# Attention scores of the later batches: float32 products on host-transposed queries and keys in place of split float16 ones

## The chip, the cores and the metric

The kernel runs on one core of a Trainium2 chip. The metric is the device time of one execution in microseconds (us), median of several runs; the kernel before has 992.15 us, from three runs between 989.74 and 999.76 us. One further execution was recorded by the hardware profiler, and all rows below come from it.

## The reference: what is computed

There are 8 batches of 8 heads, 576 tokens and 64 elements per head. Keys and values are averaged over groups of 8 tokens, which leaves 72 of each; attention over those 72 gives a 576 x 512 matrix per batch, and a feed-forward block of width 2048 follows.

```python
k_p = k.reshape(B, H, Sp, pool, D).mean(axis=3)          # pool = 8, Sp = 72
v_p = v.reshape(B, H, Sp, pool, D).mean(axis=3)
scores = scale * np.matmul(q, k_p.transpose(0, 1, 3, 2))
attn = softmax(scores)                                    # over the 72 keys
x = np.matmul(attn, v_p)                                  # heads side by side: 576 x 512
xn = (x - mu) / np.sqrt(var + 1e-06) * g_ln
out = x + np.maximum(xn @ w_ch1, 0.0) @ w_ch2             # 512 -> 2048 -> 512
```

## The kernel before, in words

The 8 x 576 = 4608 tokens are cut into 36 tiles of 128 tokens, numbered t = 0 to 35, and into 9 chunks of four tiles (512 tokens) for the feed-forward block. A batch is 4.5 tiles long, so tiles 4, 13, 22 and 31 belong to two batches each; `segments` gives the one or two ranges of a tile with their batch. These four are called split tiles below, the other 32 whole tiles.

Attention for a tile has two stages. `stage_a(t)` loads the queries of tile t+2, computes scores (`scores`), exponentials (`probs`, which ends in a DMA transpose), and, for the tiles after the first nine, prepares the queries of tile t+1 (`split_q`). `values(t)` multiplies by the pooled values, normalises, and produces the transposed input of the feed-forward block. `ffn_in` (L488) and `ffn_out` (L515) are the two large products; each is done as three float16 products over high and low parts, with a 128x512 product as the unit, and one call of either is a unit of 12 such products.

The scores have two forms. In the first two batches (tiles 0 to 8, `T32` = 9) the host has laid out the queries transposed, and L353 multiplies float32: one product takes a pair of heads, 128 rows of both heads' elements, against `kblk`, a block-diagonal 128x144 matrix with the 72 pooled keys of each head of the pair. A float32 product of the program is two matmul instructions in the trace. In the later batches (tiles 9 to 35) the queries come with tokens on the partitions. `split_q` finds the largest element of each row on VectorE (L326), derives a power of two from it (L107, L108, L114), combines it with the scale of the keys (L331), writes the high float16 part on ScalarE (L141) and the low part on VectorE (L142), and has a DMA transpose both (L335). The result lies in a `wf` buffer. Each head then takes two products, L348 with 128 rows against `KHH` and L349 with 64 rows against `KLL`, so a whole tile takes 16 matmuls and a split tile 32, where each covers 64 columns.

Keys are pooled on GpSimd by `pool_k`: L223 and L224 add halves, and the last addition goes to `kblk` in two half-height pieces (L228) for the first two batches, and to a `wf` buffer in one piece (L233) for the later ones. There `max_k` and `split_k` follow: a maximum (L237), a small matmul over all partitions (`all_max`, L129), a scale, a split, and six DMAs into the tile that serves as `KHH` and `KLL`.

`wf` is a pool of three buffers. Besides the split queries and keys, the conversion of the weights lives in it: the weights arrive in 16 blocks of 1 MB (`load_raw` into a ring of five buffers, L153), `convert` (L163 to L185) turns each into a float32 block in `wf`, and `split_w1` and `split_w2` write the high and low float16 weights from there. All transfers go through the queue of SyncE (SP).

Two things set the order. The text in `START` lists the operations up to the end of chunk 1: loads, pooling (`HK`), stage A of tiles 0 to 11 (`A`), values (`B`), weight conversion (`C`, `S1`, `M2`, `S2`) and feed-forward quarters (`I`, `O`). After it a loop over chunks 2 to 8 runs 32 feed-forward units each, with stage A of the next chunk's tiles ahead of units 0, 6, 12 and 18 (`A_AT`) and their values ahead of units 5, 11, 17 and 23 (`B_AT`); the keys and values of batch b are prepared behind the values of the last tile of batch b-2. The framework's scheduler simulates the program and may move instructions between engines' turns, so the order on an engine is not always that of the text.

Of the kernel before, what the change touches and what calls it, by code (L numbers as in the profile page):

```python
# [39 lines left out]
UNITS = 2 * NFT  # L40
B32 = 2
T32 = B32 * S // P
A_AT, B_AT = (0, 6, 12, 18), (5, 11, 17, 23)
# [16 lines left out]
@with_exitstack  # L60
def attn_ffn_kernel(ctx: ExitStack, tc: tile.TileContext, qT, q, kT, k, v, g, w1, w2, out):
    nc = tc.nc
# [21 lines left out]
    make_identity(nc, ident)  # L84
    kblk = [wk2.tile([P, NPAIR, 2 * KV], F32, name="kblk") for _ in range(B32)]
    phl = [const.tile([P, 2, H, P], F16, name=f"phl{i}") for i in range(2)]
# [9 lines left out]
    def wf_tile():  # L96
        return wk3.tile([P, NKT * WC], F32, name="wf")
# [4 lines left out]
    def scalar_tile(name, n=1):  # L102
        return small.tile([P, n], F32, name=name)
# [109 lines left out]

    KHH, KLL, CK, kst, kp, kmax, kraw = {}, {}, {}, {}, {}, {}, {}
    VA, VB, CV, vp, vmax, vraw = {}, {}, {}, {}, {}, {}

    def load_k(b, p, kr=None, queue=nc.sync):
        kraw[b, p] = kr = wk2.tile([P, POOL, KV], F32, name="kr") if kr is None else kr
        queue.dma_start(out=kr, in_=(kT[b] if b < B32 else k[b - B32])[:, p])

    def pool_k(b, p, eng):
        kr = kraw.pop((b, p))
        eng.tensor_add(out=kr[:, 0:4, :], in0=kr[:, 0:4, :], in1=kr[:, 4:8, :])  # L223
        eng.tensor_add(out=kr[:, 0:2, :], in0=kr[:, 0:2, :], in1=kr[:, 2:4, :])  # L224
        if b < B32:
            for j in range(2):
                r, c = slice(j * D, (j + 1) * D), slice(j * KV, (j + 1) * KV)
                eng.tensor_add(out=kblk[b][r, p, c], in0=kr[r, 0, :], in1=kr[r, 1, :])  # L228
        else:
            if p == 0:  # L230
                kst[b] = wf_tile()
                kp[b] = kst[b][:, 0 : NPAIR * KV].rearrange("p (a k) -> p a k", k=KV)
            eng.tensor_add(out=kp[b][:, p, :], in0=kr[:, 0, :], in1=kr[:, 1, :])  # L233

    def max_k(b):
        m = scalar_tile("mk")
        nc.vector.tensor_reduce(  # L237
            out=m, in_=kp[b], axis=AX.XY, op=ALU.max, apply_absolute_value=True
        )
        kmax[b] = all_max(m)  # L240

    def split_k(b):

        e, s = kmax.pop(b), scalar_tile("sk")
        kh, kl = (
            kst[b].bitcast(F16)[:, i * NPAIR * KV : (i + 1) * NPAIR * KV].rearrange(
                "p (a k) -> p a k", k=KV
            )
            for i in (2, 3)
        )  # L250
        kb = wk2.tile([P, NPAIR, 2 * KV], F32, name="kblk")
        kb = kb.rearrange("p a k -> p (a k)").bitcast(F16).rearrange("p (i h k) -> p i h k", i=2, k=KV)
        KHH[b], KLL[b] = kb[:, 0], kb[:D, 1]
        pow2_inverse(s, e, 13)
        CK[b] = wk3.tile([P, 1], F32, name="ck")
        nc.vector.tensor_scalar_mul(out=CK[b], in0=e, scalar1=2.0**-26 * EXP_SCALE)
        split(kp.pop(b), s, kh, kl)
        for j in range(2):
            r, hs = slice(j * D, (j + 1) * D), slice(j * NPAIR, (j + 1) * NPAIR)
            for i in range(2):  # L260
                nc.sync.dma_start(out=KHH[b][i * D : (i + 1) * D, hs, :], in_=kh[r])
            nc.sync.dma_start(out=KLL[b][:, hs, :], in_=kl[r])

# [36 lines left out]

    q_sb, ESC, E, PT, X, Z, zTs = {}, {}, {}, {}, {}, {}, {}

# [10 lines left out]
    def load_q(t):  # L313
        q_sb[t] = wk3.tile([P, NPAIR, P], F32, name="q")
        if t < T32:
            nc.sync.dma_start(out=q_sb[t], in_=qT[t])
        else:
            nc.sync.dma_start(out=q_sb[t].rearrange("p a c -> p (a c)"), in_=q[t - T32])

    def split_q(t):  # L320

        qn = q_sb.pop(t).rearrange("p a c -> p (a c)")
        flat = wf_tile().bitcast(F16)
        qhl = flat[:, 0 : 2 * DM]
        m, e, s = scalar_tile("mq"), scalar_tile("eq"), scalar_tile("sq")
        nc.vector.tensor_reduce(out=m, in_=qn, axis=AX.X, op=ALU.max, apply_absolute_value=True)  # L326
        pow2_floor(e, m)
        pow2_inverse(s, e, 13)
        ESC[t] = f = scalar_tile("esc")
        for r, b in segments(t):  # L330
            nc.vector.tensor_mul(out=f[r], in0=e[r], in1=CK[b][r])  # L331
        parts = qhl.rearrange("p (h a d) -> p h a d", a=2, d=D)
        split(qn.rearrange("p (h d) -> p h d", d=D), s, parts[:, :, 0, :], parts[:, :, 1, :])
        q_sb[t] = flat[:, 2 * DM : 4 * DM].rearrange("p (h c) -> p h c", c=P)
        nc.sync.dma_start_transpose(out=q_sb[t], in_=qhl)  # L335

    def scores(t):
# [4 lines left out]
        for half in range(2):  # L342
            ps = ps_s.tile([P, 512], F32, name="ps_s")
            for i in range(4 if t >= T32 else 0):
                h = 4 * half + i
                for r, b in segments(t):
                    o = ps[r, i * KV : (i + 1) * KV]
                    nc.tensor.matmul(o, lhsT=q[:, h, r], rhs=KHH[b][:, h, :], start=True, stop=False)  # L348
                    nc.tensor.matmul(o, lhsT=q[:D, h, r], rhs=KLL[b][:, h, :], start=False, stop=True)  # L349
            for i in range(2 if t < T32 else 0):  # L350
                p = 2 * half + i
                for r, b in segments(t):
                    nc.tensor.matmul(  # L353
                        ps[r, i * 2 * KV : (i + 1) * 2 * KV],
                        lhsT=q[:, p, r],
                        rhs=kblk[b][:, p, :],
                        start=True,
                        stop=True,
                    )
            pss.append(ps[:, : 4 * KV].rearrange("p (h k) -> p h k", k=KV))  # L360
# [11 lines left out]
    def probs(t):  # L372
        e, ph = E.pop(t), phl[t % 2]
        nc.scalar.activation(out=e, in_=e, func=AF.Exp, scale=ESC.pop(t) if t >= T32 else EXP_SCALE)
        nc.scalar.copy(  # L375
# [280 lines left out]
```

## Time and profile before

| what | before |
|---|---|
| median of 3 runs | 992.15 us (989.74 to 999.76) |
| the profiled execution, its own time | 994.91 us |
| its span, first to last instruction | 993.1 us |
| mean granted TensorE clock | 0.957 |
| TensorE matmul busy | 881.1 us (89%) |
| VectorE busy | 606.6 us (61%) |
| ScalarE busy | 294.0 us (30%) |
| GpSimd busy | 266.7 us (27%) |

In the rows, PE is TensorE's matmul side and PEld its weight loads, DVE is VectorE, ACT ScalarE, POOL GpSimd and SPq the DMA queue of SyncE. A row of a timeline has start and duration in us, engine, line, operation, output and inputs, a count when like instructions are merged, and in brackets the idle time of the engine just before with what ended it. A matmul's duration runs to its modelled end and overlaps the next one's; the distance from one start to the next is what it costs in a row of many. A row of groups has the count, the busy time and mean ns of one, and the idle time before them. A row of windows has the busy time and instruction count of PE, PEld, DVE, ACT and POOL in a stretch, then the granted TensorE clock (1.00 is full), the DMA share and GB/s.

### The profile page before, as it was taken

The page shows a single profiled execution, that of the slowest core. Times are in us where ns is not written, and L with a number is a line of the kernel's source. Part 1 is how long each engine was busy: PE and PEld are TensorE (multiplying, and loading weights), DVE is VectorE, ACT ScalarE, POOL GpSimd, SP SyncE. Part 2 cuts the span into 40 slices and gives each one's busy share as a digit, 9 for nine tenths or more (in the row PEclk, how much of TensorE's full clock was granted, in tenths as well). Part 3 has the DMA queues.
Part 4 walks back from the last instruction along what each step waited for, and adds up shares of the span by engine and source line. Part 5 has one row for each costly group of instructions (what it writes and reads, how often), then busy time and mean ns, then how long its engine had stood idle before and what let it go on. Part 6 is the DMA issues. An engine that isn't in the chain of part 4 may idle for free.

```text
span 993.1 us, 13139 instructions
## 1 busy us (share of the span) xinstructions
PE 881.1 (89%) x4826; PEld 442.8 (45%) x4826; DVE 606.6 (61%) x1540; ACT 294.0 (30%) x558; POOL 266.7 (27%) x316
## 2 busy tenths in 40 slices
PE   3135599584999999999999999999999999999998
PEld 2124346341444444445444444454444445444443
DVE  6999998858675467357636574676464435542222
ACT  3435443434322232223222222242232223210110
POOL 5865851326211623132402131211011101200000
PEclk9997799795999899999999899999998999999999
DMA  9848651533432564155324243323232212200001
GB/s 293 201 109 220 174 165 21 212 94 91 117 96 62 146 135 98 35 141 114 78 54 122 57 110 45 107 69 85 48 91 54 43 33 74 60 16 33 11 1 43
DMA packets 166001, 93.31 MB, mean 94 GB/s; under 512 B 144816, under 2 KB 148272, under 8 KB 163888
## 3 DMA queue, kind: packets, MB, share of 16 engines
q1 hardware_dynamic: 165936, 92.47, 36.4%
q8 instruction: 38, 0.62, 0.3%
q14 instruction: 27, 0.22, 0.1%
HBM read 45.09 MB, written 9.44 MB: 55 GB/s over the span
## 4 chain that ended last, share of the span: by engine, by line
PE 77%; DVE 14%; DMA 4%; issue 2%; SPq 1%; POOL 1%; ACT 1%; DVEq 0%; POOLq 0%; ACTq 0%
PE ps_f L515 35%; PE ps_f L488 34%; PE ps_s L349 3%; PE ps_s L348 3%; DVE wf L169 2%; DVE wf L166 1%; DVE w1L L142 1%; DMA q<-in_qT_dram 1%; DMA vr<-in_v_dram 1%; DVE y L458 1%; PE ps_x L413 1%; DVE a L455 1%; DVE e L365 1%; DVE wm L181 1%; PE ps_x L416 1%
## 5 line engine op out<-in xcount | busy, mean ns | idle before, releaser
L488 PE MATMUL ps_f<-zT,w1H 128*128 128x512 f16 (+1 forms) x1248 | 353.5, 368 | 6.7 <-DVE x L525 4.8
L515 PE MATMUL ps_f<-w2H,ring 128*128 128x512 f16 x1152 | 356.5, 385 | 0.8 <-DVE ring L497 0.8
L515 PEld LDWEIGHTS <-ring 128*128 128x128 f16 x1728 | 169.0, 99 | 204.2 <-issue 11.6
L488 PE MATMUL ps_f<-zT,w1L 128*128 128x512 f16 (+1 forms) x624 | 229.4, 368 | 0.0
L515 PE MATMUL ps_f<-w2L,ring 128*128 128x512 f16 x576 | 221.7, 385 | 0.0
L525 DVE SCALAR_TENSOR_TENSOR x<-ps_f,c_out,x 128x512 f32<-128x512 f32 x144 | 107.5, 748 | 137.3 <-PE ps_f L515 134.2
L488 PEld LDWEIGHTS <-w1H 128*128 128x128 f16 x1248 | 122.1, 99 | 131.7 <-issue 10.9
L497 DVE SCALAR_TENSOR_TENSOR ring<-ps_f,ring 128x512 f16<-128x512 f32 (+1 forms) x156 | 100.7, 647 | 117.5 <-ACT ring L496 116.3
L496 ACT ACTIVATE ring<-ps_f 128x512 f16<-128x512 f32 (+1 forms) x156 | 87.7, 564 | 246.4 <-PE ps_f L488 245.8
L382 POOL TENSOR_TENSOR phl<-e,phl 128x512 f16<-128x512 f32 x36 | 42.6, 1185 | 266.8 <-ACT phl L375 232.1
L488 PEld LDWEIGHTS <-w1L 128*128 128x128 f16 x624 | 62.0, 99 | 64.6 <-issue 2.2
L467 POOL TENSOR_TENSOR hl<-z,hl 128x512 f16<-128x512 f32 x36 | 42.5, 1180 | 147.5 <-ACT hl L466 140.0
L353 PE MATMUL ps_s<-kblk,q 128*128 128x144 f32 (+1 forms) x80 | 22.0, 457 | 52.0 <-issue 20.1
L436 ACT ACTIVATE x<-ps_x,rs 128x64 f32<-128x64 f32 x144 | 33.4, 315 | 115.4 <-DVE rs L427 58.6
L348 PE MATMUL ps_s<-kblk,wf 128*128 128x72 f16 (+1 forms) x240 | 50.9, 212 | 7.8 <-DMA wf<-wf 7.8
L349 PE MATMUL ps_s<-kblk,wf 64*128 64x72 f16 (+1 forms) x240 | 50.4, 210 | 0.0
L185 POOL TENSOR_TENSOR wf<-wf,ring 128x1024 f32<-128x1024 f32 x16 | 40.7, 2547 | 33.2 <-DMA ring<-in_w_dram 15.1
L363 DVE TENSOR_REDUCE mx<-ps_s 128x4 f32<-128x288 f32 x72 | 32.4, 454 | 27.9 <-PE ps_s L349 26.1
L272 POOL TENSOR_TENSOR vr<-vr 72x512 f32<-72x512 f32 x28 | 38.2, 1372 | 34.4 <-DMA vr<-in_v_dram 34.1
L466 ACT CAST hl<-z 128x512 f16<-128x512 f32 x36 | 22.3, 620 | 84.1 <-DVE z L462 84.0
L141 ACT ACTIVATE wf<-q,sq 128x512 f16<-128x512 f32 x27 | 19.6, 724 | 75.1 <-PE ps_s L349 71.5
L353 PEld LDWEIGHTS ps_s<-kblk,q 128*128 128x128 f32 (+1 forms) x80 | 16.6, 289 | 55.5 <-issue 34.7
(99 smaller groups left out, 835.7 us busy)
## 6 DMA issues: line engine op xcount, KB each, us to landing
ring<-in_w_dram SPq DMA_DIRECT2D x16, 1024.0 KB
out_dram<-x SPq DMA_DIRECT2D x36, 256.0 KB
vr<-in_v_dram SPq DMA_DIRECT2D x28, 288.0 KB
kr<-in_k_dram SPq DMA_DIRECT2D x24, 288.0 KB
q<-in_q_dram SPq DMA_DIRECT2D x27, 256.0 KB
q<-in_qT_dram SPq DMA_DIRECT2D x9, 256.0 KB
kr<-in_kT_dram SPq DMA_DIRECT2D x5, 288.0 KB
kblk<-wf SPq DMA_DIRECT2D x36, 36.0 KB
```

The costliest lines, as they stand in the source:

```text
L185: nc.gpsimd.tensor_tensor(out=w, in0=w, in1=hi.bitcast(F32), op=ALU.mult)
L272: eng.tensor_add(out=vr[:, :, 0:4, :], in0=vr[:, :, 0:4, :], in1=vr[:, :, 4:8, :])
L348: nc.tensor.matmul(o, lhsT=q[:, h, r], rhs=KHH[b][:, h, :], start=True, stop=False)
L349: nc.tensor.matmul(o, lhsT=q[:D, h, r], rhs=KLL[b][:, h, :], start=False, stop=True)
L353: nc.tensor.matmul(ps[r, i * 2 * KV : (i + 1) * 2 * KV], lhsT=q[:, p, r], rhs=kblk[b][:, p, :], start=True, stop=True,)
L382: nc.gpsimd.tensor_tensor(out=ph[:, 0, :, KA:P], in0=e[:, :, 0:KA], in1=ph[:, 0, :, 0:KA], op=ALU.subtract)
L467: nc.gpsimd.tensor_tensor(out=zhl[:, 1, :], in0=z, in1=zhl[:, 0, :], op=ALU.subtract)
L488: nc.tensor.matmul(ps, lhsT=w[:, k, fs], rhs=zT[:, kz, cols], start=(n == 0), stop=(n == 3 * NKT - 1),)
L496: nc.scalar.activation(out=h[:, 0, i, cols], in_=ps, func=AF.Relu)
L497: nc.vector.scalar_tensor_tensor(out=h[:, 1, i, cols], in0=ps, scalar=0.0, in1=h[:, 0, i, cols], op0=ALU.max, op1=ALU.subtract,)
L515: nc.tensor.matmul(ps, lhsT=h[:, j, i, cols], rhs=w[:, f, :], start=(n == 0), stop=(n == 3 * FPQ - 1),)
L525: nc.vector.scalar_tensor_tensor(out=x, in0=ps, scalar=c_out[:, q : q + 1], in1=x, op0=ALU.mult, op1=ALU.add)
```

## The change

The float16 form is taken out. The host lays out all queries and keys as it did for the first two batches, and all 36 tiles use the float32 products on `kblk`. `split_q`, `max_k` and `split_k` are gone, with their calls and the per-row scale of the exponential. There are two `kblk` tiles in all, which batches use in turn (`b % NKB`); they are allocated once, so that their zero blocks stay, and the keys of batch b overwrite those of batch b-2. `START` and the loop are unchanged.

```diff
-B32 = 2
-T32 = B32 * S // P
+NKB = 2
-    kblk = [wk2.tile([P, NPAIR, 2 * KV], F32, name="kblk") for _ in range(B32)]
+    kblk = [const.tile([P, NPAIR, 2 * KV], F32, name=f"kblk{i}") for i in range(NKB)]
...
-        queue.dma_start(out=kr, in_=(kT[b] if b < B32 else k[b - B32])[:, p])
+        queue.dma_start(out=kr, in_=kT[b][:, p])
...
-        if b < B32:
-            for j in range(2):
-                r, c = slice(j * D, (j + 1) * D), slice(j * KV, (j + 1) * KV)
-                eng.tensor_add(out=kblk[b][r, p, c], in0=kr[r, 0, :], in1=kr[r, 1, :])
-        else:
-            if p == 0:
-                kst[b] = wf_tile()
-                kp[b] = kst[b][:, 0 : NPAIR * KV].rearrange("p (a k) -> p a k", k=KV)
-            eng.tensor_add(out=kp[b][:, p, :], in0=kr[:, 0, :], in1=kr[:, 1, :])
-    def max_k(b):
...
-    def split_k(b):
...
+        for j in range(2):
+            r, c = slice(j * D, (j + 1) * D), slice(j * KV, (j + 1) * KV)
+            eng.tensor_add(out=kblk[b % NKB][r, p, c], in0=kr[r, 0, :], in1=kr[r, 1, :])
...
-        if t < T32:
-            nc.sync.dma_start(out=q_sb[t], in_=qT[t])
-        else:
-            nc.sync.dma_start(out=q_sb[t].rearrange("p a c -> p (a c)"), in_=q[t - T32])
-    def split_q(t):
...
+        nc.sync.dma_start(out=q_sb[t], in_=qT[t])
...
-            for i in range(4 if t >= T32 else 0):
-                h = 4 * half + i
-                for r, b in segments(t):
-                    o = ps[r, i * KV : (i + 1) * KV]
-                    nc.tensor.matmul(o, lhsT=q[:, h, r], rhs=KHH[b][:, h, :], start=True, stop=False)
-                    nc.tensor.matmul(o, lhsT=q[:D, h, r], rhs=KLL[b][:, h, :], start=False, stop=True)
-            for i in range(2 if t < T32 else 0):
+            for i in range(2):
                 p = 2 * half + i
                 for r, b in segments(t):
                     nc.tensor.matmul(
                         ps[r, i * 2 * KV : (i + 1) * 2 * KV],
                         lhsT=q[:, p, r],
-                        rhs=kblk[b][:, p, :],
+                        rhs=kblk[b % NKB][:, p, :],
...
-        nc.scalar.activation(out=e, in_=e, func=AF.Exp, scale=ESC.pop(t) if t >= T32 else EXP_SCALE)
+        nc.scalar.activation(out=e, in_=e, func=AF.Exp, scale=EXP_SCALE)
...
-        if T32 <= t + 1 < NTT:
-            split_q(t + 1)
...
-        if b >= B32 and p == NPAIR - 1:
-            max_k(b)
-            split_k(b)
```

More of the change, by code (lines that the diff above doesn't have):

```diff
@@ L60, in attn_ffn_kernel @@
 @with_exitstack
-def attn_ffn_kernel(ctx: ExitStack, tc: tile.TileContext, qT, q, kT, k, v, g, w1, w2, out):
+def attn_ffn_kernel(ctx: ExitStack, tc: tile.TileContext, qT, kT, v, g, w1, w2, out):
     nc = tc.nc
@@ L211, in split_w2 @@
             split(w, ws[:, i : i + 1], w2H[:, fs, :], w2L[:, fs, :])
-    KHH, KLL, CK, kst, kp, kmax, kraw = {}, {}, {}, {}, {}, {}, {}
+    kraw = {}
     VA, VB, CV, vp, vmax, vraw = {}, {}, {}, {}, {}, {}
@@ L224, in pool_k @@
         eng.tensor_add(out=kr[:, 0:2, :], in0=kr[:, 0:2, :], in1=kr[:, 2:4, :])
-        if b < B32:
-            for j in range(2):
-                r, c = slice(j * D, (j + 1) * D), slice(j * KV, (j + 1) * KV)
-                eng.tensor_add(out=kblk[b][r, p, c], in0=kr[r, 0, :], in1=kr[r, 1, :])
-        else:
-            if p == 0:
-                kst[b] = wf_tile()
-                kp[b] = kst[b][:, 0 : NPAIR * KV].rearrange("p (a k) -> p a k", k=KV)
-            eng.tensor_add(out=kp[b][:, p, :], in0=kr[:, 0, :], in1=kr[:, 1, :])
-    def max_k(b):
[L236 to L240, printed above, removed]
-    def split_k(b):
[L244 to L257, printed above, removed]
         for j in range(2):
[L259 to L262, printed above, removed]
+            r, c = slice(j * D, (j + 1) * D), slice(j * KV, (j + 1) * KV)
+            eng.tensor_add(out=kblk[b % NKB][r, p, c], in0=kr[r, 0, :], in1=kr[r, 1, :])
     def load_v(b, i, vr=None, queue=nc.sync):
@@ L298, in split_v @@
             nc.sync.dma_start(out=VB[b][KV + i * KR : KV + (i + 1) * KR], in_=vh[KA:])
-    q_sb, ESC, E, PT, X, Z, zTs = {}, {}, {}, {}, {}, {}, {}
+    q_sb, E, PT, X, Z, zTs = {}, {}, {}, {}, {}, {}
     def segments(t):
@@ L314, in load_q @@
         q_sb[t] = wk3.tile([P, NPAIR, P], F32, name="q")
-        if t < T32:
-            nc.sync.dma_start(out=q_sb[t], in_=qT[t])
-        else:
-            nc.sync.dma_start(out=q_sb[t].rearrange("p a c -> p (a c)"), in_=q[t - T32])
-    def split_q(t):
[L322 to L329, printed above, removed]
-        for r, b in segments(t):
[L331 to L335, printed above, removed]
+        nc.sync.dma_start(out=q_sb[t], in_=qT[t])
     def scores(t):
@@ L343, in scores @@
             ps = ps_s.tile([P, 512], F32, name="ps_s")
-            for i in range(4 if t >= T32 else 0):
-                h = 4 * half + i
-                for r, b in segments(t):
-                    o = ps[r, i * KV : (i + 1) * KV]
-                    nc.tensor.matmul(o, lhsT=q[:, h, r], rhs=KHH[b][:, h, :], start=True, stop=False)
-                    nc.tensor.matmul(o, lhsT=q[:D, h, r], rhs=KLL[b][:, h, :], start=False, stop=True)
-            for i in range(2 if t < T32 else 0):
+            for i in range(2):
                 p = 2 * half + i
@@ L635 @@
     lay = {
-        "qT": q[:B32].transpose(1, 3, 0, 2).reshape(NPAIR, P, T32, P).transpose(2, 1, 0, 3),
-        "q": q[B32:].transpose(0, 2, 1, 3).reshape(NTT - T32, P, DM),
-        "kT": k[:B32].reshape(B32, NPAIR, 2, KV, POOL, D).transpose(0, 2, 5, 1, 4, 3).reshape(B32, P, NPAIR, POOL, KV),
-        "k": k[B32:].reshape(B - B32, 2, NPAIR, KV, POOL, D).transpose(0, 1, 5, 2, 4, 3).reshape(B - B32, P, NPAIR, POOL, KV),
+        "qT": q.transpose(1, 3, 0, 2).reshape(NPAIR, P, NTT, P).transpose(2, 1, 0, 3),
+        "kT": k.reshape(B, NPAIR, 2, KV, POOL, D).transpose(0, 2, 5, 1, 4, 3).reshape(B, P, NPAIR, POOL, KV),
         "v": v.reshape(B, H, KV, POOL, D).transpose(0, 2, 1, 3, 4),
```

## The prediction

> **What bounds the kernel now.** I read the table of engines first, then the stretches of the span, then the timeline of TensorE around the scores.
>
> ```profile
> PE 881.1 (89%) x4826; PEld 442.8 (45%) x4826; DVE 606.6 (61%) x1540; ACT 294.0 (30%) x558; POOL 266.7 (27%) x316
> ```
> ```profile
> 100.00:184.00 84.00, 71.02 (x459) 42.45 (x458) 76.28 (x200) 38.22 (x71) 39.74 (x36) 0.91 0.47 141
> 184.00:254.20 70.20, 40.40 (x207) 21.13 (x207) 50.46 (x110) 25.08 (x38) 32.39 (x30) 0.76 0.36 105
> 254.20:880.00 625.80, 625.55 (x3431) 302.44 (x3431) 359.77 (x974) 175.74 (x353) 126.99 (x170) 0.98 0.34 81
> ```
>
> The kernel has two parts. From 254.2 us on TensorE is never idle (625.55 of 625.80 us) while VectorE works 57% of the time. Whatever leaves TensorE there leaves the end time, whatever leaves another engine does not. Before 254.2 us TensorE waits much of the time; there VectorE (76.28 of 84 us in the first of the two stretches) and single waits set the pace.
>
> ```profile
> L348 PE MATMUL ps_s<-kblk,wf 128*128 128x72 f16 x192 | 39.7, 207 | 7.8 <-DMA wf<-wf 7.8
> L348 PE MATMUL ps_s<-kblk,wf 128*64 128x72 f16 x48 | 11.2, 233 | 0.0
> ```
>
> At 8 L348 products for a whole tile and 16 for a split one, these are 24 whole and 3 split tiles. Tiles 9 and 10 run before 254.2 us, so 22 whole and all 3 split ones lie in the bound part.
>
> **Whole tiles in the bound part.**
>
> ```profile
> 508.91 0.38 PE L515 MATMUL ps_f<-w2H,ring 128*128 128x512 f16 x1
> 509.13 0.20 PE L348 MATMUL ps_s<-kblk,wf 128*128 128x72 f16 x1
> 509.25 0.20 PE L349 MATMUL ps_s<-kblk,wf 64*128 64x72 f16 x1
> ...
> 511.31 0.61 PE L488 MATMUL ps_f<-zT,w1H 128*128 128x512 f16 x2
> ```
>
> The 16 float16 products of a tile hold TensorE from 509.13 to 511.31, 2.18 us or 136 ns each, though each streams only 72 columns. The float32 form can be seen in the first tiles, at full clock and at half clock:
>
> ```profile
> 80.96 0.73 PE L353 MATMUL ps_s<-kblk,q 128*128 128x144 f32 x4
> 81.53 0.22 PE L129 MATMUL ps_f<-ident,rowmax 128*128 128x128 bf16 x1
> ```
> ```profile
> 99.18 2.26 PE L353 MATMUL ps_s<-kblk,q 128*128 128x144 f32 x8 [4.46 <-DVE e L365]
> 101.23 0.26 PE L413 MATMUL ps_x<-va,pt 128*128 128x65 f16 x1
> ```
> ```profile
> 80.90:82.40 1.50, 1.40 (x12) 1.14 (x10) 0.74 (x3) 1.47 (x2) 0.75 (x1) 1.00 1.06 393
> 99.10:101.30 2.20, 2.12 (x9) 2.07 (x10) 2.20 (x5) 2.17 (x7) 0.64 (x1) 0.50 1.17 268
> ```
>
> Half a tile is 4 instructions and takes 0.57 us at full clock, so a tile takes at most 1.14 us. A whole tile takes 2.05 us at clock 0.50, which is 1.03 us at full clock. I take 1.06, since the start-up of the second half overlaps in an unbroken row. The first weight load should hide behind the 128x512 product ahead of it, whose slot is 0.22 us (508.91 to 509.13). Gain: 2.18 - 1.06 = 1.12 us a tile, times 22 = **24.6 us**, with ends 22 x 1.04 = 22.9 and 22 x 1.15 = 25.3.
>
> [...]
>
> **Split tiles, and the clock behind them.**
>
> ```profile
> 333.37 0.22 PE L348 MATMUL ps_s<-kblk,wf 128*64 128x72 f16 x1
> ...
> 338.39 0.61 PE L515 MATMUL ps_f<-w2H,ring 128*128 128x512 f16 x1
> ```
> ```profile
> 337.30:344.10 6.80, 6.80 (x20) 2.71 (x21) 3.76 (x9) 3.56 (x8) 3.85 (x5) 0.50 0.20 48
> 344.10:548.90 204.80, 204.60 (x1142) 99.37 (x1139) 120.81 (x334) 57.89 (x117) 54.38 (x75) 1.00 0.40 97
> 548.90:555.70 6.80, 6.80 (x24) 2.96 (x24) 2.34 (x7) 2.75 (x4) 0.67 (x1) 0.50 0.23 51
> 760.60:767.30 6.70, 6.70 (x24) 3.06 (x24) 2.99 (x10) 0.72 (x1) 0.00 (x0) 0.50 0.18 40
> ```
>
> A split tile takes 5.02 us (333.37 to 338.39). What I did not expect: each of the three is followed by 6.8 us at half clock, the only such stretches in the bound part (20.3 us at half clock are 1.6% of 625.8 us, as its mean of 0.98 has it), though PE is shown busy throughout (6.80 of 6.80). So the narrow products, 64 columns wide for 5 us, seem to let the clock fall; the whole tiles, 2.18 us, do not. In the first case 1.1 us of the half-clock stretch lies in the tile itself and 5.7 behind it, costing 2.85 us; I take 2.5 us for each, together **7.5 us**, with ends 0 (it stays) and 3 x 3.4 = 10.2 (all of it).
>
> ```profile
> 53.53 1.67 PE L353 MATMUL ps_s<-kblk,q 128*64 128x144 f32 x10 [15.93 <-issue]
> 55.13 0.23 PE L413 MATMUL ps_x<-va,pt 128*128 128x65 f16 x1
> ```
> ```profile
> L353 PE MATMUL ps_s<-kblk,q x10: 444/446/503, 53.5 to 54.8; 128*64 128x144 f32 x10
> L353 PE MATMUL ps_s<-kblk,q x8: 447/447/580, 99.2 to 101.0; 128*128 128x144 f32 x8
> ```
>
> In float32 a split tile has 16 instructions. Ten of tile 4's took 1.60 us, 0.16 each against 0.256 for a whole tile's at half clock, and their duration (446 ns) is that of the half-clock ones (447), so the two segments ran side by side in part. At full clock 16 take 16 x 0.08 = 1.3 us; without that overlap 2 x 1.14 = 2.3, with perfect overlap 1.1. Gain 3 x (5.02 - 1.3) = **11.2 us**, ends 8.2 and 11.8. A stretch this short should no longer bring the clock down.
>
> **The opening, before 254.2 us.** Here the preparation that goes away matters.
>
> ```profile
> 219.12 0.72 ACT L141 ACTIVATE wf<-q,sq 128x512 f16<-128x512 f32 x1 [1.60 <-PE ps_s L349]
> 226.80 0.24 PE L348 MATMUL ps_s<-kblk,wf 128*128 128x72 f16 x1 [7.77 <-DMA wf<-wf]
> 229.68 1.13 ACT L163 ACTIVATE wf<-ring 128x1024 f32<-128x1024 f32 x1 [1.77 <-PE ps_s L349]
> 238.62 2.15 DVE L331 TENSOR_TENSOR esc<-eq,ck 64x1 f32<-64x1 f32 x1
> 240.70 0.13 DVE L108 TENSOR_SCALAR rowmax<-rowmax 128x1 int32<-128x1 int32 x1
> 240.89 0.29 PE L129 MATMUL ps_f<-ident,rowmax 128*128 128x128 bf16 x1 [11.25 <-DVE rowmax L108]
> ```
>
> Tile 10's split waits for tile 9's scores to free a `wf` buffer, then its transpose keeps TensorE idle 7.77 us. The third weight conversion waits in turn for tile 10's scores (229.68), and VectorE's L331 stands right ahead of the `rowmax` that ends the next wait of 11.25 us. Without the split, tile 10 waits only until VectorE has read tile 9's scores out of the two score banks, some 2.2 us after them: 5.6 us come free, and the conversions lose that delay too.
>
> ```profile
> L326 DVE TENSOR_REDUCE mq<-q 128x1 f32<-128x512 f32 x5 | 3.4, 674 | 2.0 <-DMA q<-in_q_dram 2.0
> L331 DVE TENSOR_TENSOR esc<-eq,ck 128x1 f32<-128x1 f32 x4 | 2.5, 657 | 0.0
> L331 DVE TENSOR_TENSOR esc<-eq,ck 64x1 f32<-64x1 f32 x1 | 2.1, 2145 | 0.0
> L142 DVE SCALAR_TENSOR_TENSOR wf<-q,sq,wf 128x512 f16<-128x512 f32 x2 | 1.7, 838 | 0.5 <-ACT wf L141 0.5
> ```
>
> Between 100 and 254 us these rows make 9.7 us of VectorE work that goes; the small ones around them and those of the keys add some 3.5. About half of the 13 lie where VectorE is the bound: 5.4 us. I take 5.6 + 5.4 = **11 us**. The ends are wide, since the scheduler draws a new order for this part: 5.6 + 13 = 19 if all of it counts, and a loss of 10, one more wait of the size of the 11.25 above, if the new order is worse.
>
> **What costs nothing.** The queries and keys are loaded in the same sizes. SP's queue loses 27 transposes and 36 small DMAs and gains none, so what stands behind them (weights, values, the transposes of `probs`) can only go earlier. GpSimd's last addition becomes two:
>
> ```profile
> L233 POOL TENSOR_TENSOR wf<-kr 128x72 f32<-128x72 f32 x24 | 7.7, 335 | 56.2 <-PE ps_s L349 49.9 <-DVE y L458 3.2 <-DVE w1L L142 3.1
> L228 POOL TENSOR_TENSOR kblk<-kr 64x72 f32<-64x72 f32 x10 | 4.2, 424 | 0.4
> ```
>
> That is 24 x (2 x 0.424 - 0.335) = 12.3 us more, under GpSimd's idle time (126.99 of 625.8 us busy). New is that these additions wait for the last scores of batch b-2, with the low parts of `probs` and of the normalised tile behind them on GpSimd; but they are issued behind that tile's values, so the scores are long done. If that cover were gone, the wait would be one tile's scores, 1 us. VectorE and ScalarE lose work in the bound part, where neither bounds.
>
> **The sum.** On the profiled execution, 994.91 us (span 993.1): 994.91 - 24.6 - 11.2 - 7.5 - 11 = 940.6 us. The median of the runs shown, 992.15, is 2.8 lower, so I forecast **938 us**.
>
> **Rivals.** (A) The forecast, 62%; alone it ranges from 927 to 949. (B) The opening gains nothing, because the new order puts other waits there: 949 us, 16%; for it speaks that VectorE stays loaded there with weight conversion. (C) Float32 split tiles let the clock fall as before: 938 + 7.5 = 945.5 us, 8%; against it, they are shorter than the whole float16 tiles, which do not. (D) The opening loses 10 us by one more wait: 959 us, 7%. (E) Nothing else comes free, the bound part falls in with another engine and only the opening gains: 994.91 - 11 - 2.8 = 981 us, 4%; against it, VectorE is at 57% there and ScalarE lower. (F), the slower side: float32 products count as idleness for the clock, so that every tile is followed by a half-clock stretch. Such a stretch is 6.8 us and costs 3.4; 22 whole tiles pay 75 us, the clock gain of 7.5 is lost, and the result is 938 + 75 + 7.5 = 1020 us. It decides once more than about 16 of the 22 tiles pay ((24.6 + 11.2 + 7.5 + 11) / 3.4). For it: at 99 us float32 runs at 0.50. Against it: TensorE had been idle 4.46 us just before, and at 80.9 the clock held 1.00. 3%. [...]
>
> **How the numbers follow.** The extreme ends give 992.15 - 25.3 - 11.8 - 10.2 - 19 = 926 and 992.15 - 22.9 - 8.2 - 0 + 10 = 971. The range 922 to 957 holds A, B, C and a little more than the best sum, and leaves out D, E and F, 14%, with something for tails. A measurement of this kernel can tell about 1% from no change. A to D and E (981 is 1.1% less) are faster; of E I give a quarter to no change. Faster 0.96, same 0.01, slower 0.03.
>
> **What would show it.** Right: a whole tile's L353 products last 1.0 to 1.15 us from their start to the next line's; split tiles 1.1 to 2.3; no half-clock stretch behind 260 us; the bound part starts near 243 us in place of 254. Wrong: 0.50 clock behind tiles, idle PE in the bound part, `rowmax` waits of the old sum in the opening.

## The result, and the profile after

The changed kernel takes 951.88 us (median of 4 runs, 951.54 to 953.08), the kernel before on the same chip 994.65 (4 runs, 989.74 to 999.76). The ratio is 0.957, with a 95% interval of 0.952 to 0.963. The forecast was 938, its range 922 to 957. The profiled execution took 951.54 us; its span is 949.7, 43.4 shorter than before.

First the row of the engines and the stretches of the changed kernel, with the same columns as before. Its score products are in L292, the feed-forward products in L427 (`ffn_in`) and L454 (`ffn_out`); in the kernels of the experiments these numbers shift by a few lines.

```profile
PE 837.1 (88%) x4580; PEld 426.9 (45%) x4580; DVE 551.9 (58%) x1333; ACT 268.4 (28%) x525; POOL 277.5 (29%) x340
```
```profile
170.00:203.00 33.00, 10.50 (x72) 8.75 (x71) 29.66 (x73) 16.76 (x26) 17.22 (x16) 0.57 0.57 159
...
247.80:258.40 10.60, 0.11 (x2) 0.05 (x2) 10.48 (x18) 1.35 (x2) 8.63 (x6) 0.60 0.00 0
258.40:263.70 5.30, 5.30 (x14) 1.95 (x15) 3.19 (x6) 2.19 (x2) 0.00 (x0) 0.50 0.00 0
263.70:880.00 616.30, 615.99 (x3354) 298.88 (x3353) 311.88 (x799) 152.56 (x323) 121.29 (x162) 1.00 0.28 68
```

TensorE is busy 44.0 us less (881.1 to 837.1), and the span is 43.4 us shorter: the time it waits stayed what it was, 112 us of span without a matmul in both. The bound part now begins at 258.4 us and not at 254.2, although a whole group of VectorE's work is gone. From 263.7 us on the clock is 1.00 without a break.

Next a whole tile and a split tile of the changed kernel, in the timeline of TensorE:

```profile
405.80 0.38 PE L454 MATMUL ps_f<-w2H,ring 128*128 128x512 f16 x1
406.01 1.14 PE L292 MATMUL ps_s<-kblk,q 128*128 128x144 f32 x8
406.99 0.59 PE L427 MATMUL ps_f<-zT,w1H 128*128 128x512 f16 x2
```
```profile
529.35 0.38 PE L427 MATMUL ps_f<-zT,w1L 128*128 128x512 f16 x1
529.66 1.20 PE L292 MATMUL ps_s<-kblk,q 128*64 128x144 f32 x16
530.79 0.39 PE L454 MATMUL ps_f<-w2H,ring 128*128 128x512 f16 x1
```

The whole tile holds TensorE for 0.98 us (2.18 before), the split one for 1.13 us (5.02 before). From the product ahead to a split tile it is 0.31 us where a whole tile has 0.21; that was so in the kernel before too (333.06 to 333.37).

The opening is another matter. These are the matmuls of the changed kernel that TensorE began after a wait of over 4 us, between 170 and 205 us:

```profile
177.71 1.30 PE L292 MATMUL ps_s<-kblk,q 128*128 128x144 f32 x4 [4.79 <-DVE e L304]
...
189.19 2.26 PE L292 MATMUL ps_s<-kblk,q 128*128 128x144 f32 x8 [7.72 <-issue]
195.45 2.19 PE L292 MATMUL ps_s<-kblk,q 128*64 128x144 f32 x16 [4.00 <-issue]
202.46 0.59 PE L427 MATMUL ps_f<-zT,w1H 128*128 128x256 f16 x2 [4.83 <-DMA zT<-hl]
```

Tile 10's old wait for its transposed queries (7.77 us) is gone. But from 172.9 to 202.5 us TensorE has only scores to do, of tiles up to 13 that the scheduler pulled ahead, and then waits for `zT`, the last quarter of chunk 1's transposed input. That quarter comes from tile 7's normalisation on VectorE. Its first and last steps, before:

```profile
156.82 0.69 DVE L440 BATCH_NORM_STATS2 st<-x 128x6 f32<-128x512 f32 x1 [0.40 <-ACT x L436]
...
162.14 0.54 DVE L462 TENSOR_SCALAR z<-x,mv,y 128x512 f32<-128x512 f32 x1
```

And in the changed kernel, with two of the instructions that stand between them:

```profile
168.59 0.68 DVE L379 BATCH_NORM_STATS2 st<-x 128x6 f32<-128x512 f32 x1
...
177.48 2.18 DVE L394 SCALAR_TENSOR_TENSOR a<-y,ve 128x1 f32<-128x1 f32 x1
...
185.65 2.48 DVE L141 SCALAR_TENSOR_TENSOR w1L<-wf,gs,w1H 128x256 f16<-128x256 f32 x1
...
193.38 1.31 DVE L401 TENSOR_SCALAR z<-x,mv,y 128x512 f32<-128x512 f32 x1
```

From the statistics to `z` it was 5.3 us and is 24.8. The statistics themselves come 11.8 us later than before (168.6 against 156.8); what delayed them was not followed up. What lies between is seen in VectorE's groups of that stretch of the changed kernel (168.5 to 193.4 us):

```profile
L141 DVE SCALAR_TENSOR_TENSOR w1L<-wf,gs,w1H 128x256 f16<-128x256 f32 x8 | 6.5, 824 | 0.0
L168 DVE SCALAR_TENSOR_TENSOR wf<-wf,ring 128x1024 int32<-128x1024 int32 x3 | 3.6, 1213 | 0.0
L165 DVE TENSOR_SCALAR_CACHE_REDUCE wf<-wf 128x1024 f32<-128x1024 f32 x3 | 3.6, 1207 | 0.0
L164 DVE TENSOR_SCALAR ring<-ring 128x1024 int32<-128x1024 int32 x4 | 2.7, 672 | 0.0
L394 DVE SCALAR_TENSOR_TENSOR a<-y,ve 128x1 f32<-128x1 f32 x3 | 2.6, 866 | 0.0
L304 DVE TENSOR_TENSOR e<-ps_s,mx 128x288 f32<-128x288 f32 x6 | 2.6, 445 | 0.0
L302 DVE TENSOR_REDUCE mx<-ps_s 128x4 f32<-128x288 f32 x6 | 2.6, 446 | 0.0
```

Weight conversion (L164, L165, L168, L141) takes 16.4 us of it, maxima and differences of scores that were pulled ahead 5.2, both put between the small steps of one normalisation. No row has idle time in front of it: VectorE was busy, though two of its instructions took some 2 us longer than their like (last section), but not with the work TensorE stood waiting for. That `wf` buffers which no query occupies any more, and scores that need no preparation, gave the scheduler more that was ready to be put there is a guess: a kernel below that keeps its split queries in `wf` has the same lateness.

### The profile page after: what moved, and what is told of

Same layout as the page of the kernel before. It is cut to its first block, busy times and chain, and to the rows that moved or that the text cites. A ratio compares the mean times of both kernels' runs of the same rounds, so it can differ in the third digit from the quotient of the medians.

```text
span 949.7 us, 12332 instructions
## 1 busy us (share of the span) xinstructions
PE 837.1 (88%) x4580; PEld 426.9 (45%) x4580; DVE 551.9 (58%) x1333; ACT 268.4 (28%) x525; POOL 277.5 (29%) x340
## 4 chain that ended last, share of the span: by engine, by line
PE 76%; DVE 16%; DMA 2%; POOL 2%; issue 2%; ACT 1%; SPq 1%; DVEq 0%; ACTq 0%; POOLq 0%
PE ps_f L454 37%; PE ps_f L427 35%; PE ps_s L292 2%; DVE w1L L141 2%; DVE wf L168 2%; DVE a L394 1%; DVE wf L165 1%; PE ps_x L352 1%; DVE e L304 1%; DVE y L397 1%; DMA ring<-in_v_dram 1%; DVE mx L302 1%; DVE ring L436 1%; PE ps_x L355 1%; DVE ring L164 1%
## 5 line engine op out<-in xcount | busy, mean ns | idle before, releaser
L454 PE MATMUL ps_f<-w2H,ring 128*128 128x512 f16 x1152 | 355.1, 383 | 3.8 <-DVE ring L436 3.8
L427 PE MATMUL ps_f<-zT,w1H 128*128 128x512 f16 (+1 forms) x1248 | 351.4, 367 | 5.6 <-DMA zT<-hl 4.8
L454 PEld LDWEIGHTS <-ring 128*128 128x128 f16 x1728 | 169.1, 99 | 204.8 <-issue 10.6
L427 PE MATMUL ps_f<-zT,w1L 128*128 128x512 f16 (+1 forms) x624 | 228.7, 367 | 0.0
L454 PE MATMUL ps_f<-w2L,ring 128*128 128x512 f16 x576 | 220.4, 383 | 0.0
L427 PEld LDWEIGHTS <-w1H 128*128 128x128 f16 x1248 | 122.7, 99 | 129.3 <-issue 8.2
L292 PE MATMUL ps_s<-kblk,q 128*128 128x144 f32 (+1 forms) x320 | 57.2, 348 | 69.1 <-issue 32.9
L427 PEld LDWEIGHTS <-w1L 128*128 128x128 f16 x624 | 61.8, 99 | 64.2 <-issue 1.1
L292 PEld LDWEIGHTS ps_s<-kblk,q 128*128 128x128 f32 (+1 forms) x320 | 48.7, 218 | 77.7 <-issue 55.2
L313 ACT ACTIVATE e<-e 128x576 f32<-128x576 f32 x36 | 24.6, 682 | 140.3 <-DVE e L304 116.2
L184 POOL TENSOR_TENSOR wf<-wf,ring 128x1024 f32<-128x1024 f32 x16 | 39.9, 2492 | 36.6 <-DVE wm L176 24.6
L237 POOL TENSOR_TENSOR vr<-vr 72x512 f32<-72x512 f32 x28 | 36.7, 1322 | 43.3 <-DMA vr<-in_v_dram 42.6
L314 ACT CAST phl<-e 128x1024 f16<-128x1024 f32 x36 | 37.5, 1042 | 3.5 <-DMA pt<-phl 2.9
L394 DVE SCALAR_TENSOR_TENSOR a<-y,ve 128x1 f32<-128x1 f32 x108 | 34.3, 317 | 3.3 <-DMA vb<-vh 0.7
L304 DVE TENSOR_TENSOR e<-ps_s,mx 128x288 f32<-128x288 f32 x72 | 30.5, 444 | 4.7 <-POOL phl L324 4.7
```

Of the source, the lines that this page charges most:

```text
L184: nc.gpsimd.tensor_tensor(out=w, in0=w, in1=hi.bitcast(F32), op=ALU.mult)
L292: nc.tensor.matmul(ps[r, i * 2 * KV : (i + 1) * 2 * KV], lhsT=q[:, p, r], rhs=kblk[b % NKB][:, p, :], start=True, stop=True,)
L304: nc.vector.tensor_tensor(out=e[:, hs, :], in0=sc, in1=mx[:, hs].unsqueeze(2).broadcast_to([P, 4, KV]), op=ALU.subtract,)
L314: nc.scalar.copy(out=ph[:, :, :, 0:KA], in_=e[:, :, 0:KA].unsqueeze(1).broadcast_to([P, 2, H, KA]))
L394: nc.vector.scalar_tensor_tensor(out=a, in0=y, scalar=ve, in1=y, op0=ALU.mult, op1=ALU.mult)
L427: nc.tensor.matmul(ps, lhsT=w[:, k, fs], rhs=zT[:, kz, cols], start=(n == 0), stop=(n == 3 * NKT - 1),)
```

## The experiments

First in question was whether the scores that were pulled ahead had taken the opening's gain, and with it the price of the two forms of product. Times are medians; ratios are to the kernel before on the same chip.

**Scores held back (two kernels).** The order of the score products is pinned to that of the text, from tile 12 or from tile 9 on, so that none is pulled ahead.

```diff
-                    nc.tensor.matmul(
+                    mm = nc.tensor.matmul(
...
+                    if t >= HOLD:
+                        tc.keep_in_program_order(mm)
```

> The changed kernel, with the score products of tiles 12 and later kept in the order of the program text on TensorE, so that the scheduler cannot move them ahead of the opening's feed-forward units. Theory (the opening gained nothing because four tiles' scores were pulled into it, with their query loads ahead of the last weight block in SP's queue): the last weight block is issued near 210 us in place of 230.7, the 10.5 us wait of TensorE for rowmax shrinks to under 4, and the time falls by 8 to 15 us to 937 to 944. Rival (the opening is bound by VectorE and weight conversion, idle time only changes its place): 949 to 954.

> The same with tiles 9 and later. Theory: as with tiles 12 and later, 935 to 945; the scores of 9 to 11 are needed soon, so holding them gains at most another 2 us. Rival: 949 to 954.

Measured: 958.45 us from tile 12 on (ratio 0.963, 0.960 to 0.967) and 956.71 from tile 9 on (0.962, 0.959 to 0.965). Neither is faster than the changed kernel. The wait that the pulled scores had stood in now lies open, in TensorE's timeline of the first kernel and of the second:

```profile
202.63 0.58 PE L430 MATMUL ps_f<-zT,w1H 128*128 128x256 f16 x2 [19.71 <-DMA zT<-hl]
```
```profile
193.60 0.58 PE L430 MATMUL ps_f<-zT,w1H 128*128 128x256 f16 x2 [23.19 <-DMA zT<-hl]
```

So that theory fell. Held from tile 12 on, the feed-forward products resume as late as in the changed kernel (202.6 us against 202.5): the scores had filled a wait that is there without them. Held from tile 9 on, the products resume 8.9 us earlier and the bound part begins at 252.2 us, but it then takes 698.9 us in place of 691.35, with the held scores and another wait of 3.1 us for `zT` in it, and the time does not fall. The wait's end, `zT<-hl`, pointed to tile 7's normalisation.

**The float16 form with even rows.** In the kernel before, the product of the low key part gets 128 rows, the lower half zero, so that L349's products have 128 rows like L348's (L350 and L349 here).

```diff
-        KHH[b], KLL[b] = kb[:, 0], kb[:D, 1]
+        KHH[b], KLL[b] = kb[:, 0], kb[:, 1]
+        nc.vector.memset(kb[D:, 1], 0.0)
...
-                    nc.tensor.matmul(o, lhsT=q[:D, h, r], rhs=KLL[b][:, h, :], start=False, stop=True)
+                    nc.tensor.matmul(o, lhsT=q[:, h, r], rhs=KLL[b][:, h, :], start=False, stop=True)
```

> The kernel before, with the low float16 product of each head given 128 rows in place of 64 (the lower half of its keys is zero), so that all score products have one row count. Theory (the 136 ns per product come from the alternation of 128 and 64 rows): a whole tile falls from 2.18 to 0.5 to 0.7 us, a split tile from 5.2 to about 1.2, no half-clock stretch is left in the bound part, and the time falls by 50 to 58 us to 935 to 945. Rival (a product of this size costs 136 ns whatever its rows): 988 to 998, half-clock stretches stay.

Measured: 966.67 us (ratio 0.972, 0.969 to 0.976). A whole tile in the timeline of TensorE, first and last product, and what follows it:

```profile
517.79 0.20 PE L349 MATMUL ps_s<-kblk,wf 128*128 128x72 f16 x1
...
518.27 0.20 PE L350 MATMUL ps_s<-kblk,wf 128*128 128x72 f16 x1
518.31 0.60 PE L489 MATMUL ps_f<-zT,w1H 128*128 128x512 f16 x2
```

The 16 products take 0.52 us, 32 ns each instead of 136. What made the float16 form dear was the alternation of 128 and 64 rows, not float16: with even rows it costs half of the float32 tile's 0.98 us. By its size a switch costs about 136 - 32 = 104 ns. It is paid both ways, since in the kernel before the starts lie 0.14 us apart from a product of 64 rows to one of 128 and back (509.25, 509.39, 509.53). What the time goes to can be seen in part in the weight loads (PEld), with alternating rows in the kernel before, then with even rows in this one:

```profile
509.52 0.09 PEld L349 LDWEIGHTS <-wf 64*128 64x128 f16 x1
509.53 0.20 PE L349 MATMUL ps_s<-kblk,wf 64*128 64x72 f16 x1
```
```profile
517.82 0.10 PEld L349 LDWEIGHTS <-wf 128*128 128x128 f16 x1
517.85 0.20 PE L349 MATMUL ps_s<-kblk,wf 128*128 128x72 f16 x1
```

With even rows a load begins one product ahead of its own, with alternating rows only with its own, so that its 0.09 to 0.10 us no longer hide. Not every change of the row count does this: in the kernel before, products of 128 and of 88 rows alternate 0.03 us apart, with the loads ahead:

```profile
300.29 0.10 PEld L416 LDWEIGHTS <-pt 88*128 88x128 f16 x1
300.32 0.19 PE L416 MATMUL ps_x<-vb,pt 88*128 88x65 f16 x1
```

Why a load begins late at the switch between 128 and 64 rows and not at that between 128 and 88, no run here shows.

The expectation of 935 to 945 us was missed by over 20. The bound part is not the reason: from the same product on (254.2 us before, 275.6 here) it takes 689.1 us instead of 738.9, less than in the changed kernel although four tiles' more scores lie in it. The granted clock has a mean of 0.99 from 262 to 400 us and of 1.00 in the three stretches from there to 880; from 485.1 to 880 us TensorE waits 2.67 us (392.23 of 394.90 busy). The loss of 21.4 us lies in the opening, where `zT` is late in its timeline too:

```profile
202.26 0.58 PE L489 MATMUL ps_f<-zT,w1H 128*128 128x256 f16 x2 [28.51 <-DMA zT<-hl]
```

**Float32 products doubled.** In the changed kernel every score product is issued twice.

```diff
+                    for _ in range(2):
-                    nc.tensor.matmul(
+                        nc.tensor.matmul(
...
```

> The changed kernel with every float32 score product issued twice with the same result. Theory (in the bound part each microsecond of TensorE is a microsecond of the end): 0.98 us more for each of some 20 whole tiles there and 1.1 for each split one, and more in the opening: 972 to 982 us; clock stays at 1.00 behind 270 us, also behind split tiles of 2.1 us. Rival (score products lie in slack): 950 to 954. Rival (float32 products count as idleness for the clock): half-clock stretches appear behind tiles, above 1000.

Measured: 975.75 us (ratio 0.982, 0.980 to 0.985), 23.9 us over the changed kernel. A doubled whole tile and a stretch with many of them:

```profile
690.83 2.12 PE L293 MATMUL ps_s<-kblk,q 128*128 128x144 f32 x16
692.79 0.59 PE L428 MATMUL ps_f<-zT,w1H 128*128 128x512 f16 x2
```
```profile
580.00:900.00 320.00, 320.00 (x1760) 161.81 (x1758) 144.46 (x361) 74.97 (x154) 37.45 (x49) 1.00 0.22 53
```

A tile takes 1.96 us, twice 0.98, and a split one 2.17 instead of 1.13. The 19 whole and 2 split tiles that lie in the bound part of both kernels make 19 x 0.98 + 2 x 1.04 = 20.7 us of the 23.9; the rest lies ahead of them, where other tiles' scores are doubled. So what TensorE is given there appears in the end time about one for one. The stretch of 320 us with its doubled tiles has clock 1.00, so rows of float32 products of up to 2.17 us do not let it fall. Rivals C and F are out.

**What the clock falls behind.** The three half-clock stretches of the kernel before remained unexplained: narrow products or alternating rows? One run of each of two kernels: the padded one with the split tiles' products issued eight times, and the kernel before with four whole tiles' products issued three times. Both products of a head are in the added loop, of which the lines show the first.

```diff
+                    for _ in range(8 if len(segments(t)) > 1 else 1):
-                    nc.tensor.matmul(o, lhsT=q[:, h, r], rhs=KHH[b][:, h, :], start=True, stop=False)
+                        nc.tensor.matmul(o, lhsT=q[:, h, r], rhs=KHH[b][:, h, :], start=True, stop=False)
...
+                    for _ in range(3 if t in (17, 20, 26, 29) else 1):
-                    nc.tensor.matmul(o, lhsT=q[:, h, r], rhs=KHH[b][:, h, :], start=True, stop=False)
+                        nc.tensor.matmul(o, lhsT=q[:, h, r], rhs=KHH[b][:, h, :], start=True, stop=False)
...
```

> The padded float16 kernel (966.7 us), with the score products of the split tiles 13, 22 and 31 each issued eight times: narrow 128x64 products without any alternation of row counts, for about 5 us (8 x 0.647) in a row, as long as the split tiles of the kernel before. Theory one (the alternation of 128 and 64 rows, kept up for 5 us, is what let the clock fall behind the three split tiles): no half-clock stretch behind them, and the time grows by 3 x 7 x 0.65 = 13.6 us alone, to 979 to 983 us. Theory two (64 columns for 5 us let it fall, however they are fed): each is followed by some 6.8 us at 0.50.

> The kernel before (994 us), with the score products of four whole tiles (17, 20, 26, 29) each issued three times: alternating 128 and 64 rows over all 128 columns for 6.5 us in a row instead of 2.18. Theory one (alternation kept up for 5 us lets the clock fall): a stretch of some 6.8 us at 0.50 behind each of these four too, and the time grows by 4 x 4.4 + 4 x 3.4 = 31 us, with the spread of the opening's new order on top. Theory two (it takes the 64 columns of the split tiles): no half-clock stretch behind the four, and 17.5 us more.

Measured, one run each: 981.65 and 1020.81 us (before: 993.06). A long narrow tile with even rows and the stretch behind it, in the first kernel; then the first of the long alternating tiles up to the fall and the fall itself, and the fall behind the last of the four, in the second:

```profile
553.80:560.80 7.00, 7.00 (x258) 6.89 (x258) 4.48 (x16) 1.70 (x5) 2.36 (x4) 1.00 0.03 6
560.80:600.00 39.20, 39.20 (x241) 18.69 (x240) 22.82 (x68) 10.72 (x20) 8.80 (x12) 1.00 0.51 106
```
```profile
432.80:438.30 5.50, 5.50 (x42) 3.68 (x40) 2.13 (x5) 0.93 (x4) 0.00 (x0) 1.00 0.14 51
438.30:445.10 6.80, 6.80 (x22) 2.78 (x22) 2.46 (x10) 2.74 (x4) 1.42 (x2) 0.50 0.29 63
...
745.50:752.30 6.80, 6.80 (x26) 3.08 (x26) 2.38 (x9) 2.74 (x4) 0.95 (x1) 0.50 0.17 39
```

6.9 us of narrow products at 27 ns each (256 in the first of these rows, with as many weight loads) leave the clock at 1.00; 5.5 us of alternating ones over all 128 columns (from 432.82 us on) bring it to 0.50 for 6.8 us. Such stretches, of 6.8 to 6.9 us at 0.50 or 0.51, begin at 438.3, 520.2, 663.5 and 745.5 us, as many as there are long tiles. It is the alternation of 128 and 64 rows, and it takes longer than one whole tile's 2.18 us. The growth of 27.8 us lies under the 31 that were expected.

**Tile 7's normalisation put first.** Now the new theory of the opening. Operations of `START` that come behind tile 7's values (`B.7`) are kept behind its `z` with the framework's `issue_after`, which ties VectorE's instructions alone (the expectation's "on every engine" is wrong). Three kernels: six tokens; the three conversions alone; the three stages A alone.

```diff
-        nc.vector.tensor_scalar(
+        ZI[t] = nc.vector.tensor_scalar(
             out=z, in0=x, scalar1=mv[:, 0:1], scalar2=y, op0=ALU.subtract, op1=ALU.mult
-        )
+        ).ins
...
-        ops[name](*map(int, args))
+        if token in ('C.2.4', 'C.2.5', 'C.1.6', 'A.9', 'A.10', 'A.11'):
+            with tc.issue_after(ZI[7]):
+                ops[name](*map(int, args))
+        else:
+            ops[name](*map(int, args))
```

> The changed kernel (951.9 us), with the weight conversions C.2.4, C.2.5, C.1.6 and the stages A.9 to A.11 of the opening's plan kept, on every engine, behind tile 7's subtraction and product (L402, tile z): VectorE then issues 26 short instructions between tile 7's bn_stats (L379) and its z, where the changed kernel has 54, long ones of the conversions among them. Theory (the opening lost what it had gained because VectorE reaches tile 7's z 25 us behind its bn_stats, against 5 us before): z follows within 12 us, TensorE's wait between 172.9 and 202.5 us of the changed kernel shrinks by 12 to 20 us, and the time is 937 to 945 us. Rival (the opening is bound by the sum of VectorE's work, whatever its order): the wait only moves to a later place, and the time is 949 to 955 us.

> As the run with the six tokens held behind tile 7's z, but only the three conversions C.2.4, C.2.5 and C.1.6 held; the stages A.9 to A.11 stay free. 30 instructions of VectorE stand between tile 7's bn_stats and z. Theory: the conversions are the long ones, so that it gains nearly the same, 938 to 946 us, and the pulled-ahead score products still fill what is left of TensorE's wait. Rival (total of VectorE's work): 949 to 955 us.

> The changed kernel with only the stages A.9 to A.11 held behind tile 7's z; the three conversions C.2.4, C.2.5 and C.1.6 stay free. 37 instructions of VectorE stand between tile 7's bn_stats and z, the conversions' 1 to 2 us ones among them. Theory (the conversions are what delays z): z comes 15 us or more behind bn_stats and the time is 945 to 954 us. Rival (the maxima and differences of the score products that were pulled ahead delay it): z within 10 us of bn_stats and 936 to 942 us, as with the conversions held.

Measured: 935.73 us with all six held (ratio 0.941, 0.938 to 0.943), 937.63 with the conversions alone (0.943, 0.940 to 0.946), 948.74 with the stages A alone (0.956, 0.954 to 0.957). With all six, tile 7's steps and TensorE's wait are:

```profile
166.56 0.69 DVE L379 BATCH_NORM_STATS2 st<-x 128x6 f32<-128x512 f32 x1 [0.21 <-ACT x L375]
...
171.78 0.54 DVE L401 TENSOR_SCALAR z<-x,mv,y 128x512 f32<-128x512 f32 x1
```
```profile
178.99 0.61 PE L427 MATMUL ps_f<-zT,w1H 128*128 128x256 f16 x2 [8.36 <-DMA zT<-hl]
```
```profile
229.80:240.70 10.90, 0.03 (x3) 0.04 (x1) 10.90 (x17) 2.89 (x4) 10.61 (x12) 0.68 0.23 76
240.70:932.30 691.60, 687.50 (x3678) 331.99 (x3678) 339.02 (x839) 161.12 (x336) 130.26 (x175) 1.00 0.26 63
```

`z` follows the statistics by 5.2 us, the feed-forward products resume at 179.0 us instead of 202.5, and the bound part starts at 240.7 instead of 258.4 with 691.6 us behind it, as in the changed kernel (949.7 - 258.35 = 691.35). The whole gain is in the opening. The conversions are nearly all of it: with them alone `z` is 9.0 us behind, with the stages A alone 17.3 us. All six and the conversions alone differ by 1.9 us; both times lie just under the ranges that were expected.

**Controls for the hold.** The same six tokens held in the padded float16 kernel and in the kernel before.

> The kernel before with the low key product padded to 128 rows (lower half zero), as in the padded run (966.7 us), and the same six tokens held behind tile 7's z. The padded run lost 28.5 us of TensorE's time waiting at 173.8 to 202.3 us for tile 7's transposed result. Theory (this wait comes from the order of VectorE's instructions too): the wait shrinks by 10 to 20 us and the time is 947 to 957 us, about the float32 form's 951.9 us, although split float16 stays. Rival (the float16 form's opening is bound by the sum of its VectorE work): 963 to 969 us.

> Control: the kernel before, split float16 scores unchanged, with the same six tokens of the opening's plan held behind tile 7's z as in the run of the changed kernel that took 935.7 us. Theory (the hold only gives back an order that the kernel before has already: there z follows bn_stats by 5.3 us): the time stays within 985 to 999 us, no gain of over 1%. Rival (the hold is an improvement of its own, which any of these kernels would take): 974 to 982 us, as the changed kernel went from 951.9 to 935.7 us.

Measured: 953.58 us (ratio 0.959, 0.956 to 0.962) in the padded kernel, 13 us less than without the hold; 998.65 us (1.005, 1.003 to 1.007) in the kernel before, half a per cent slower than without. TensorE's wait for `zT` in the one, then in the other:

```profile
188.36 0.58 PE L489 MATMUL ps_f<-zT,w1H 128*128 128x256 f16 x2 [12.86 <-DMA zT<-hl]
```
```profile
185.79 0.59 PE L488 MATMUL ps_f<-zT,w1H 128*128 128x256 f16 x2 [13.62 <-DMA zT<-hl]
```

So the lateness is not a matter of float32: the padded kernel, whose queries and keys are still split, has it too (`z` 22.4 us behind, 5.4 with the hold). And the hold is no improvement of its own: the kernel before had tile 7's statistics at 156.8 us and `z` 5.3 us later, and with the hold the scheduler's new order brings the statistics only at 170.5 us, `z` 8.5 us behind them, and makes a wait where there was none. Each of these edits, however small, draws the opening anew.

**The query loads kept in order.** On top of the six tokens, the query loads of tiles 12 and later are pinned in SP's program order, against the second wait of the opening.

```diff
-        nc.sync.dma_start(out=q_sb[t], in_=qT[t])
+        ld = nc.sync.dma_start(out=q_sb[t], in_=qT[t])
+        if t >= 12:
+            tc.keep_in_program_order(ld)
```

> The changed kernel with the six tokens held behind tile 7's z, and the query loads of tiles 12 and later kept in program order on SP, so that the last blocks of the weights are not queued behind a query load that waits for a buffer that score products free. Theory with the second half (TensorE's 10.5 us wait at 247.9 to 258.4 us, on the last block's maximum, comes from that queue): another 5 to 10 us under the run without it, 930 to 940 us. Rival one (the second wait is bound by VectorE's conversions, not by the load): within 2 us of the run without it. Rival two (only VectorE's sum counts): 949 to 955 us.

Measured: 940.97 us (ratio 0.946, 0.943 to 0.949), 5.2 us slower than without the pin; none of the three expectations. The waits between 165 and 265 us, of TensorE and of SP's queue:

```profile
PE ps_f L128 <- DVE rowmax L107: 13.5, 1, 13.5
```
```profile
SPq L333 <- POOL phl L326: 22.8, 2, 18.7
```

The queue now waits for transposes of `probs` (L333) instead of for query buffers, the last weight block is issued at 216.0 us (213.0 without the pin), and TensorE's second wait is 13.5 us in place of 10.9. In the kernel without the pin VectorE is busy for all of that wait (10.90 of 10.90 us, above). That speaks for VectorE's conversions as its limit, but no run took work out of that stretch, so it is argued and not shown.

## Why the prediction came out as it did

The time lies in the range, and the sum stands 14 us below it: three of its terms came nearly as forecast, the fourth not at all. Without that fourth term the sum is 994.91 - 24.6 - 11.2 - 7.5 = 951.6, and the profiled execution took 951.54. So close an agreement is luck in part: the whole and the split tiles gave 1.8 and 1.0 us more than forecast, and a half-clock stretch that was not in the sum took 2.65 back.

**Whole tiles: right, a little small.** 2.18 - 0.98 = 1.20 us a tile and not 1.12, 26.4 us for 22 tiles, over the upper end of 25.3. The 1.03 us that half-clock rows gave was the better bound; that it still held the start-up of a row that began after an idle time is likely, not shown. The prediction rested on the 2.18 us as measured; the padded kernel shows what they went to: the float16 form paid for its alternating rows, 136 ns a product where even rows take 32, or 0.52 us a tile.

**Split tiles: right, a little small.** The three took 5.02, 5.25 and 5.33 us before, the later two longer because more of them lay at half clock, and 1.13 us after: 3.89, 4.12 and 4.20, together 12.2 us. The forecast was 11.2 with an upper end of 11.8, as it took 5.02 for all three and 1.3 for the new form. Sixteen instructions of half the columns in 1.13 us against 0.98 for eight fit the reading that the two segments run side by side, but would fit as well if a narrow product simply cost less.

**The clock: right.** No half-clock stretch follows a split tile any more, and the experiments gave the reason: it was the alternation, not the 64 columns that the prediction named ("the narrow products, 64 columns wide for 5 us, seem to let the clock fall"). Its forecast held because the new form removes the alternation; the split tiles' products are still 64 columns wide, in a row of 1.13 us. The size was right too: 5.7, 4.8 and 4.4 us of the three stretches lay behind the tiles, a cost of 7.5 us. What it did not list is the 5.3 us at half clock with which the bound part now starts, behind the wait of 10.5 us; they cost 2.65.

The bound part as a whole: 993.1 - 254.2 = 738.9 us before, 949.7 - 258.35 = 691.35 after. Four tiles' scores (11 to 14, 3 x 0.98 + 1.13 = 4.1 us) only moved into the opening. 738.9 - 691.35 - 4.1 = 43.5 us, where the three terms made 43.3. Measured term by term it is 26.4 + 12.2 + 7.5 - 2.65 = 43.4.

**The opening: wrong.** The forecast was a gain of 11 us; it starts 4.2 us later with 4.1 us of foreign scores in it, which is nothing. The step that failed is "I take 5.6 + 5.4 = 11 us". Its first half was seen rightly, tile 10's wait is gone. But it counted VectorE's freed time and the freed buffers as time for what TensorE waits for. In the scheduler's new order weight conversions stand ahead of tile 7's `z` instead, and the feed-forward products wait. Why it chose that order is open: the padded kernel, in which no buffer came free, has it too. This is rival B, a new order that puts other waits there (949, with 16%), with a place that the prediction did not know. That the order alone is at fault is shown by the hold: with nothing added or taken away the time is 935.7 us, the bound part unchanged, the opening 13.5 us shorter than before. The 11 us were there to be had.

Rivals C and F fell with the doubled products; D would have needed a loss of 10 us in the opening, E that the bound part gains nothing. The range held the time because it left room for rival B; the measured time lies outside the 927 to 949 us of the forecast's own theory (A).

The fastest of all kernels here is the changed one with the six tokens held, 935.73 us. On its chip the kernel before took 994.38 us; the changed kernel without the hold, on another, 951.88.

## What to carry to other kernels

Where one engine is never idle, sum its products and the stretches at a lower clock, and nothing else: that sum was 43.3 us here against 43.5 measured, though errors of its terms cancelled in part. Where several engines wait for each other, work that goes away is not time: ask which step ends the wait that stands there, and whether the scheduler will give the freed engine to that step or to something else that is ready; a gain that does not appear is looked for in the order of the instructions before it is looked for in their number.

## What the hardware showed that was not expected

A switch between products of 128 and of 64 rows cost some 104 ns each here (136 ns against 32 for a product of 72 columns), and a few microseconds of such alternation brought the clock to 0.50 for 6.7 to 6.9 us although PE is shown busy throughout (6.80 of 6.80 us behind the first split tile before); the fall came 3.0 to 3.9 us after the first product of the split tiles before, and 5.5 us after that of the first long tile. Narrow products with even rows, 6.9 us of them, left it at 1.00. What it is in the alternation that brings the clock down, no run here shows.

The opening had a second thing: two of VectorE's instructions in front of `z`, quoted above, took 2.18 us (128 elements of one column; its like takes 0.21) and 2.48 us (0.47). GpSimd's rows in the changed kernel stand beside them in time:

```profile
177.26 2.38 POOL L184 TENSOR_TENSOR wf<-wf,ring 128x1024 f32<-128x1024 f32 x1 [2.79 <-DVE wm L176]
...
185.48 2.36 POOL L184 TENSOR_TENSOR wf<-wf,ring 128x1024 f32<-128x1024 f32 x1
```

Both VectorE instructions begin within 0.3 us of one of GpSimd's and end with it or 0.3 us later (179.66 and 179.64; 188.13 and 187.84). That they waited for GpSimd's there, some 2 us each, is the author's reading of this nearness in time; no run tested it. If it holds, the conversions delayed `z` twice, by their own steps and by GpSimd's part of them. The two excesses (2.18 - 0.21 and 2.48 - 0.47) are 4.0 us of the 24.8; what the time would be without them was not tried.
